# An attention and feed-forward kernel: decay rows in one stacked tile, a K=128 bias matmul for two heads, and a schedule written out as tokens

## The chip, the cores and the metric

The kernel runs on one core of a Trainium2 chip. The metric is the device time of one execution in microseconds (us), lower is better. The span of a profile (first to last instruction) is shorter than the device time of the same run (before: 415.4 against 417.08). In the text, PE is the matmul engine, DVE the vector engine, ACT the scalar engine, POOL the engine that issues the loads of q, k, v and weights, SP the engine that issues most of the other DMAs. The granted clock is the share of its full clock at which PE was allowed to run; "half clock" is a share of 0.5. Warming matmuls are matmuls on constant data that only keep PE busy. A slot is the tile that holds q and k of four heads; `widen` and `narrow` are the two feed-forward layers.

## The reference

Causal attention with a decay bias over 8 batches, 8 heads, 576 positions and 64 dimensions per head, followed by a low-rank mix along the sequence and a feed-forward layer with residual.

```python
scores = (q @ k.T) / sqrt(64)
cum = cumsum(maximum(s, 0), axis=-1)
bias = -(cum[:, :, :, None] - cum[:, :, None, :])
scores = where(causal_mask, -1e9, scores + minimum(bias, 0))
attn = softmax(scores);  x = (attn @ v) with heads side by side     # (8, 576, 512)
h = x.T @ U @ V                                                     # rank 32, along the sequence
u = x + h.T
out = u + maximum(u @ w_ch1, 0) @ w_ch2                             # 512 -> 2048 -> 512
```

## The kernel before

Per head, the scores are matmuls over 68 rows: 64 of q and k and 4 "decay rows" that carry the bias (three bf16 parts of `cum` on k's side against ones, and `-cum` against one). The decay rows of all 64 heads are made by one chain of vector operations at the start. Those of batch 0 are sent to the slots by DMA, those of later batches go through HBM.

```python
# ... s of all 64 heads, one row each: 64 partitions, 144 KB
nc.sync.dma_start(out=s_sb, in_=s.rearrange("b h s -> (b h) s"))
# ... loads of the first q and k are issued on gpsimd
spin(10)                                     # warming matmuls, 512 columns each
nc.vector.tensor_scalar(s_sb, s_sb, 0.0, 1.0 / scale, op0=ALU.max, op1=ALU.mult)
nc.vector.tensor_tensor_scan(cum, s_sb, s_sb, 0.0, op0=ALU.add, op1=ALU.max)
nc.scalar.copy(hi, upper(cum))
nc.vector.tensor_sub(rest, cum, upper(cum))
nc.scalar.mul(rows[:, 3, 0, :], cum, -1.0)
nc.vector.tensor_sub(lo, rest, upper(rest))
nc.vector.tensor_copy(mid, upper(rest))
# ...
for h in range(H):                           # rows of batch 0 into the slots
    send(nc.scalar if h in (1, 3) else nc.sync, h)
```

The rest is generators. Attention of a pair of heads (`scores`, `values`, `mix`) yields at fixed places, and at a given rate a step of feed-forward work is put in there: a quarter of `narrow`'s row block or one of `widen`'s 16 blocks, four 512-column matmuls each. A group of 512 tokens has 32 such steps.

```python
def place(g):                                # q and k of heads 16 and up, four heads at a time
    fetch_rows(g)
    # ... 4 x nc.vector.transpose on (128 x 576), then DMAs to the slot

def attend(n, rate):                         # n: pair of heads
    if n < NP:
        run(scores(n), rate)                 # 4 steps put in
    if n > 2 * PB:
        run(values(n - 1), rate)             # 2 steps
        run(mix(n - 1), rate)                # 1 step: U at once after the values of the same pair
        if hp == 0:
            fill.append(widen(b - 1))

def rest():
    for n in range(2 * PB, NP + 1):
        # ...
        if hp % 2 == 0 and n // 2 + 1 < NP // 2:
            place(n // 2 + 1)                # four transposes in a row on DVE
        attend(n, 1.0)
        if hp == 0:
            fill.append(narrow(b - 1))
```

The opening (batch 0) runs without feed-forward work, with 40 warming matmuls in all; batch 1 runs at rate 0.5 beside the first feed-forward group.

The softmax here doesn't subtract the row's maximum and nothing guards it: scores larger than these inputs give would overflow.

## Time and profile before

| | before |
|---|---|
| device time, median (first three runs) | 416.95 us |
| all runs of it in this study | 413 to 421 us, one at 427 |
| PE busy, of the span | 93% |
| first score matmul | 13.9 us |
| first feed-forward matmul ("first widen") | 44.5 us |
| first score of pair 8 (end of batch 1) | 98.2 us |
| last matmul | 411.4 us |

The page of the profile gives PE's busy tenths in 40 slices of 10.4 us, and the granted clock in tenths.

```profile
PE   7688888899889899999899999999999999999996
...
PEclk9689969999999999999999999999999999999999
```

PE is nearly full from the fifteenth slice (145 us) on. What can be gained lies before that, in idle time and in the slices of low clock. The clock records have two stretches at half: 13.7 to 23.9 and 54.6 to 61.5 us. The records begin only at 6.9 us, and the views count the time before as full; but the first ten warming matmuls start 0.43 us apart and those from 6.86 us on 0.22 us apart, so PE was at half clock until then as well.

The windows view, cut at the three stages (opening, batch 1, rest), has in its columns the length, the busy time of each engine (instructions in brackets), the granted clock, the time of all DMA packets as a share of 16 engines' time (packets overlap, so it can exceed 1) and GB/s.

```profile
core 0: us, PE busy (x) PEld busy (x) DVE busy (x) ACT busy (x) POOL busy (x), PEclk, DMA share, GB/s
0.00:44.51 44.51, 34.16 (x366) 22.04 (x373) 23.63 (x52) 22.79 (x41) 29.94 (x49) 0.88 1.48 160
44.51:98.19 53.68, 47.17 (x422) 27.01 (x429) 28.94 (x59) 24.44 (x49) 28.39 (x44) 0.94 1.25 114
98.19:411.40 313.21, 304.24 (x2548) 170.87 (x2596) 140.73 (x314) 151.94 (x296) 49.64 (x82) 1.00 0.42 74
```

The first stage has 10 us of PE idle, the second 6.5. About 2% of the matmul records are missing in this trace (3335 matmuls against 3396 weight loads), so PE's busy times are a little low, those of the last stage included.

The list of PE's waits (total, how often, longest; us):

```profile
PE pwork L308 <- DVE x_sb L293: 9.2, 8, 1.4
PE pscore L227 <- DMA slot<-hT: 3.5, 1, 3.5
PE pwork L328 <- DVE ux L317: 2.4, 10, 0.7
PE pscore L227 <- ACT pT L241: 2.1, 2, 1.1
```

L308 is the first matmul of the mix, which waits for the division that writes x_sb. Five of its eight waits, 6.1 us, lie in the last stage. The timeline of the opening (start, length, engine, line, what; in square brackets the idle time before and its releaser). From timelines only the lines that matter are shown, here and below:

```profile
0.80 0.59 SPq L444 DMA_DIRECT2D hT<-in_s_dram  x1
3.56 0.45 DVE L474 TENSOR_SCALAR hT<-hT 64x576 f32<-64x576 f32 x1
5.50 0.45 PE L166 MATMUL pwork<-identity,hT 72*128 72x72 bf16 x4
13.93 0.61 PE L227 MATMUL pscore<-slot 68*128 68x128 bf16 x4 [3.50 <-DMA slot<-hT]
```

The first score matmul stands 3.50 us for the rows' DMA, at 13.93.

### The profile page before, as it was taken

How to read it: one execution, taken by the hardware profiler on the slowest of the kernel's cores; microseconds unless marked ns; L12 is line 12 of the kernel's file. 1: busy time of each engine (PE TensorE's matmuls, PEld its weight loads, DVE VectorE, ACT ScalarE, POOL GpSimd, SP SyncE). 2: the span in 40 equal slices, each digit the busy share in tenths (PEclk: the TensorE clock that was granted, in tenths of full speed). 3: DMA queues.
4: the chain of work that ended last, by engine and by line, in shares of the span. 5: the costliest groups of instructions: out<-in, count | busy, mean ns of one | idle time of the engine just before them, and what ended most of it. 6: DMA issues, size and time to landing. Idle time of an engine off the chain costs nothing.

```text
span 415.4 us, 8407 instructions
## 1 busy us (share of the span) xinstructions
PE 385.6 (93%) x3335; PEld 219.9 (53%) x3396; DVE 194.0 (47%) x425; ACT 199.2 (48%) x386; POOL 108.0 (26%) x173
## 2 busy tenths in 40 slices
PE   7688888899889899999899999999999999999996
PEld 3456454555555455555556555565556544444442
DVE  7344355458867557474665843444344401001011
ACT  3373866505762367535663476337743450530610
POOL 8774367347563644053004000000000000000000
PEclk9689969999999999999999999999999999999999
DMA  7999999999986995379119311210001002001002
GB/s 109 189 161 178 195 115 111 74 87 189 233 132 102 180 156 73 71 96 171 28 36 127 100 41 30 69 58 11 2 27 52 25 2 76 28 14 63 25 25 76
DMA packets 76077, 36.75 MB, mean 88 GB/s; under 512 B 61382, under 2 KB 67814, under 8 KB 76038
## 3 DMA queue, kind: packets, MB, share of 16 engines
q0 software_dynamic: 65584, 18.44, 48.9%
q1 hardware_dynamic: 10438, 17.76, 14.2%
q8 instruction: 26, 0.43, 0.4%
q14 instruction: 13, 0.11, 0.1%
q10 hardware_dynamic: 16, 0.02, 0.0%
HBM read 37.51 MB, written 9.95 MB: 114 GB/s over the span
## 4 chain that ended last, share of the span: by engine, by line
PE 66%; DMA 11%; DVE 10%; issue 5%; POOL 4%; ACT 2%; SPq 1%; DVEq 0%; ACTq 0%; POOLq 0%
PE pwork L377 24%; PE pwork L361 23%; PE pscore L227 7%; PE pwork L283 5%; DVE turned L194 4%; DMA qk_sd<-in_k_dram 3%; DMA w_sb<-in_moe_w_ch_dram 2%; DMA slot<-turned 2%; DMA uT<-in_k_dram 2%; PE pwork L308 2%; DVE x_sb L293 2%; PE pwork L388 2%; DVE slot L175 1%; DMA v_slot<-in_v_dram 1%; PE pwork L337 1%
## 5 line engine op out<-in xcount | busy, mean ns | idle before, releaser
L361 PE MATMUL pwork<-uT,w_sb 128*128 128x512 bf16 x548 | 143.0, 382 | 2.0 <-ACT hT L368 0.4
L377 PE MATMUL pwork<-w_sb,hT 128*128 128x512 bf16 x550 | 138.3, 379 | 1.3
L368 ACT ACTIVATE hT<-pwork 128x512 bf16<-128x512 f32 x144 | 88.5, 614 | 83.0 <-PE pwork L361 82.8
L227 PE MATMUL pscore<-slot 68*128 68x128 bf16 (+4 forms) x576 | 70.9, 247 | 7.6 <-DMA slot<-hT 3.5
L241 ACT ACTIVATE pT<-pscore 128x512 bf16<-128x512 f32 x64 | 38.8, 606 | 81.3 <-PE pscore L227 70.7
L361 PEld LDWEIGHTS <-w_sb 128*128 128x128 bf16 x576 | 51.2, 98 | 48.3 <-issue 5.2
L377 PEld LDWEIGHTS <-hT 128*128 128x128 bf16 x576 | 51.2, 97 | 48.1 <-issue 2.1
L227 PEld LDWEIGHTS <-slot 68*128 68x128 bf16 x576 | 43.8, 100 | 38.2 <-issue 5.7
L397 DVE COPY o_sb<-pwork 128x512 f32<-128x512 f32 x36 | 24.8, 688 | 78.7 <-PE pwork L388 78.6
L194 DVE STREAM_TRANSPOSE turned<-qk_sd 128x576 bf16<-128x576 bf16 x48 | 50.3, 1119 | 5.2 <-DMA slot<-turned 2.8
L220 DVE TENSOR_TENSOR pT<-pT,keep 128x512 bf16<-128x512 bf16 (+1 forms) x84 | 27.6, 352 | 46.6 <-ACT pT L241 41.7
L249 ACT ACTIVATE pT<-pscore 128x512 bf16<-128x512 f32 x64 | 39.4, 615 | 13.5 <-PE pscore L227 13.5
L283 PEld LDWEIGHTS <-pT 128*128 128x128 bf16 x960 | 36.8, 98 | 12.7 <-issue 1.1
L253 ACT ACTIVATE pT<-pscore 128x512 bf16<-128x512 f32 x64 | 39.7, 620 | 3.3 <-PE pscore L227 3.3
L131 POOL DMA_DIRECT2D v_slot<-in_v_dram x32 | 28.2, 901 | 45.3 <-PE pwork L283 42.8
L283 PE MATMUL pwork<-v_slot,pT 128*128 128x65 bf16 x960 | 39.3, 194 | 0.7 <-DVE uT L348 0.3
L123 POOL DMA_DIRECT2D qk_sd<-in_q_dram x48 | 27.1, 576 | 47.5 <-DVE turned L194 31.5
L348 DVE CAST uT<-pwork 128x512 bf16<-128x512 f32 x30 | 20.7, 689 | 26.0 <-PE pwork L340 26.0
L293 DVE TENSOR_TENSOR x_sb<-pwork,rec 128x320 bf16<-128x320 f32 x64 | 31.3, 489 | 2.1
L123 POOL DMA_DIRECT2D qk_sd<-in_k_dram x48 | 27.2, 578 | 12.8 <-DMA w_sb<-in_moe_w_ch_dram 7.7
L292 DVE RECIPROCAL rec<-pwork 128x5 f32<-128x5 f32 x64 | 11.8, 185 | 33.9 <-PE pwork L283 33.8
L308 PE MATMUL pwork<-x_sb,U_sb 128*128 128x128 bf16 x160 | 14.4, 220 | 9.2 <-DVE x_sb L293 9.2
(65 smaller groups left out, 216.4 us busy)
## 6 DMA issues: line engine op xcount, KB each, us to landing
out_dram<-o_sb SPq DMA_DIRECT2D x36, 256.0 KB
slot<-turned SPq DMA_DIRECT2D x96, 72.0 KB
w_sb<-in_moe_w_ch_dram POOLq DMA_DIRECT2D x8, 512.0 KB, 13.6
v_slot<-in_v_dram POOLq DMA_DIRECT2D x32, 128.0 KB, 5.8
qk_sd<-in_q_dram POOLq DMA_DIRECT2D x48, 72.0 KB, 3.9
qk_sd<-in_k_dram POOLq DMA_DIRECT2D x48, 72.0 KB, 4.7
uT<-in_q_dram POOLq DMA_DIRECT2D x2, 288.0 KB, 10.4
uT<-in_k_dram POOLq DMA_DIRECT2D x2, 288.0 KB, 11.2
```

The costliest lines, as they stand in the source:

```text
L123: nc.gpsimd.dma_start(out=qk_t[g][ds(32 * a, 32), c, :].rearrange("p (n f) -> p n f", n=6), in_=src[g // 2, 4 * (g % 2) + a].rearrange("(n ...
L131: nc.gpsimd.dma_start(out=vt[:, t, :, 0:D], in_=v[b, :, ds(t * 128, 128), :].rearrange("h p d -> p h d"),)
L194: nc.vector.transpose(turned[:, e, c].rearrange("p (n m t) -> p n t m", n=6, t=3), src[:, c].rearrange("p (n t e d) -> p e n t d", n=6, t= ...
L227: nc.tensor.matmul(dst, lhsT=kT[:, ds(j * 128, 128)], rhs=qT[:, lo:hi], start=start, stop=stop, skip_group_check=not stop,)
L241: nc.scalar.activation(pT[:, hh, 0:512], diag, EXP, scale=scale)
L249: nc.scalar.activation(pT[:, hh, 512:1024], far, EXP, scale=scale)
L253: nc.scalar.activation(pT[:, hh, 1024:1536], mid, EXP, scale=scale)
L283: nc.tensor.matmul(po[:, i, :], lhsT=pT[:, hh, ds(spot(j, i), 128)], rhs=vt[:, j, h, :], start=(j == 0), stop=(j == i), skip_group_check=True,
L293: nc.vector.tensor_tensor(x_sb[:, :, ds(h * D, D)], po[:, :, 0:D], rec.to_broadcast([128, 5, D]), op=ALU.mult,)
L361: nc.tensor.matmul(f1, lhsT=w1_sb[nf // 4][:, kt, ds(nf % 4 * 128, 128)], rhs=uT[:, kt, ds(g * 512, 512)], start=(kt == 0), stop=(kt == 3),)
L368: nc.scalar.activation(hT[:, nf, :], f1, RELU)
L377: nc.tensor.matmul(f2, lhsT=hT[:, nf, ds(i * 128, 128)], rhs=w2_sb[nf // 4][:, nf % 4, :], start=(nf == 0), stop=False, skip_group_check=True,
```

## The change

The intent, as the diff shows it: heads 0 and 1 need not wait for the DMA of their decay rows, because a second matmul over all 128 rows of a stacked tile (4 parts x 32 heads) adds their bias from where the chain leaves it; the chain of heads 32 to 63 is split off and runs later; and the order of everything is written as a list of tokens, so that divisions, mixes and transposes can stand where nothing waits for them. Cut to its core:

```diff
-    TP, TT = 72, 8
+    TP, TT = 96, 6                      # fold of q and k of heads 0 to 15
+    FR = 4 * H
+    def load_decays(i, s_sb):           # 32 heads, four times: 128 partitions, 288 KB
+        nc.sync.dma_start(
+            out=s_sb,
+            in_=bass.AP(s..., i * FR * S, [[0, 4], [S, FR], [1, S]]),
+        )
+    def decays(rows, s_sb, cum):
+        blk = [ds(i * FR, FR) for i in range(4)]
+        # ... the same operations on 128 partitions; part i is written to block i
+    def product(h, dst, j, lo, hi, start, stop):
+        bias = bias_0 if h < 2 else None
+        rows = D if bias else KA
+        nc.tensor.matmul(dst, lhsT=head_of(h)[0:rows, ds(S + j * 128, 128)], ...)
+        if bias:                        # K=128: all parts, this head picked by rhs
+            nc.tensor.matmul(dst, lhsT=bias[0][:, ds(j * 128, 128)],
+                             rhs=bias[1 + h][:, lo:hi], ...)
... (cut)
-        spin(10)                        # 40 warming matmuls in all; 16 after ("p8" twice)
... (cut)
+    SEQ = (
+        "p8 T0 tA0 tV0 T1 tA1 tV1 p8 | Z0 D0 d0 T2 tV2 tV2 E0 f0 m0 D1 d1 T3 tV3 tV3 E1 f1 m1 "
... (cut)
+        "r R3 L0 D8 d8 F r E8 k8 f8 m8 T12 tV12 tV12 D9 d9 F r E9 k9 f9 m9 l4 K4 T13 tV13 "
+        "tA13 F r F r D10 d10 F r E10 k10 f10 m10 T14 tV14 tV14 D11 d11 F r E11 k11 f11 m11 "
... (cut)
+    PAIR = (
+        "D0 d0 U-2 uV-2 X-2 F r E0 k0 f0 G1 m0 F r D1 d1 Y-2 yV-2 F r E1 k1 f1 G1 m1 l0 F r "
+        "A-2 K0 a-2 F r A-1 a-1 F r F r F r "
+    )
```

Tokens: D, E are score matmuls of a head, d, f, m, l its exps; T transposes of a head, tA and tV their copies on ACT or DVE; A values and a their division; U, X, Y parts of a pair's mix and u, y their copies; G one DVE transpose of a later group; F one feed-forward step and r its relu or output copy; L the later decay chain; p warming matmuls. In PAIR the numbers count from the present pair: A-2 and A-1 are the two heads of the pair before, U-2 is the mix of two pairs before. PAIR holds 8 steps F, where the generators took 7 per pair.

## The prediction

> **What bounds it now.** TensorE. The windows view gives it 9.9 of every 10 us busy from 150 us on, at full clock; the last 80 us are feed-forward matmuls alone. It is below that before 150 us: busy 7.5, 6.5, 8.6, 8.6, 8.3 and 7.6 us in the first six tens. PE's list of waits sums to 23 us: 9.2 us of the low-rank mix (L308) on x_sb, 3.5 on the decay rows' DMA, 2.4 on ux, 2.1 on an exp, 1.3 on a slot copy. The granted clock is half in two stretches, about 13.8 to 24.0 and 54.7 to 61.5 us. The Trainium skill, "TensorE: Matmul & The Clock Gate", Part 1, says the clock halves after an idle window of about 3.4 us; the trace agrees: the first stretch begins after 3.5 us of waiting for the rows.
>
> Three stages in the timeline: opening (batch 0) to 44.5, batch 1 with the first feed-forward group 44.5 to 98.2, then 313 us to the last matmul at 411.4.
>
> **What changes.**
> 1. Heads 0 and 1 take the bias from SBUF by a K=128 matmul and wait for no row DMA. It adds 2 x 1600 columns, about 1.4 us of PE at the traced 216 ns per 512 columns. The decay chain (ready at 7.4 us) gains a few small DVE operations. First scores should start near 9.5 instead of 13.9 us.
> 2. But values of head 0 need batch 0's v, whose last load (issued 17.2, 7.1 to landing) is there at 24.3; the load order is kept. They ran at 29.3; now PE, in order, stops there until about 24.5, perhaps with its clock halved again. So about 5 us of gain survive.
> 3. Behind that come about 11 us of PE work, 9.5 of ACT and 12.6 of DVE (0.8 us per head copy, 0.67 per division). I put the first widen at 40 us (37 to 43), against 44.5. Fewer warming matmuls (16, not 40) help.
> 4. Batch 1 with 32 feed-forward steps is about 41 us of PE work (32 x 0.87, plus the rest) and took 53.7. Mixes move behind other matmuls, divisions ahead of copies; I expect 43: 10 us saved, and no half-clock stretch.
> 5. Afterwards U comes two pairs late, so x_sb is ready, and the 1.1 us stream transposes no longer stand before divisions. That removes about 6 us of L308 waits after 98 us. PE work is unchanged.
> 6. A new cost: steady pairs take 8 feed-forward steps, not 7. Counting tokens, the 32 in stock after the sequence are used up in pairs 8 to 11; pair 12 and the first two steps of 13 find none. Pair 12 is then limited by DVE (about 5.8 us against 3.1 of PE). I charge 3 to 5 us, more if the clock halves.
> 7. Later decays: about 5 us of DVE at the end of batch 1, 1 us seen by PE.
>
> **Sum.** 40 + 43 + (313 - 6.5 + 4 + 1) + 4 = 398.5; I say 398 us, 8 in 10 between 390 and 407. Chances: faster 0.93, same 0.05, slower 0.02.
>
> **What would show it.** First score matmul by 10 us; a PE wait of 3 to 6 us for v before 25 us; first widen 37 to 43; batch 1 done at 80 to 86; L308's waits under 2 us; a PE gap of 3 to 5 us around 120 to 130 without feed-forward matmuls; a dense end as before.
>
> **What would make it wrong.** The v wait absent, or costing a long half-clock stretch; rows of heads 2 to 7 landing late; DVE order stalling PE in batch 1; ACT falling behind with 8 steps; the decay chain blocking ACT.

## The result and the profile after

The changed kernel takes 411.88 us (median of 4 runs, 411.83 to 411.92); the kernel before 417.59 (4 runs). The ratio is 0.986, with a 95% interval of 0.983 to 0.989. A ratio here is the mean time of one kernel's fast runs over that of the other's of the same rounds, so it is not quite the ratio of the medians. Repeated, the same kernel gave 412.29. The gain is 1.4%, which by the mark of 2% counts as the same time (the prediction gave that 0.05); 398 us had been predicted.

The page after:

```profile
PE   5999888989999799999999999999999999999996
...
PEclk9858999999999889999999999999999999999999
```

The windows of the three stages after (columns as before):

```profile
0.00:45.74 45.74, 37.63 (x345) 23.14 (x346) 27.02 (x58) 20.72 (x39) 28.64 (x48) 0.81 1.62 165
45.74:94.06 48.32, 42.84 (x413) 25.32 (x412) 27.89 (x62) 24.55 (x49) 23.39 (x38) 1.00 0.90 109
94.06:406.09 312.03, 308.19 (x2602) 174.06 (x2600) 152.64 (x320) 153.88 (x298) 55.34 (x88) 0.99 0.51 77
```

| stage | before | predicted | after |
|---|---|---|---|
| opening, to the first widen | 44.5 | 40 | 45.7 |
| batch 1, to the first score of pair 8 | 53.7 | 43 | 48.3 |
| rest, to the last matmul | 313.2 | 311.5 | 312.0 |

The opening is no shorter. Batch 1 gained half of what was expected. Of its 5.4 us, 0.9 is work that moved: before pair 8 the traces have 128 weight loads of the feed-forward layers in the kernel before and 124 in the changed one, so one step of 32 (0.87 us by the prediction) went from batch 1 to the rest. The rest came out as the sum said, but, as will be seen, by two errors that cancel. The prediction's sum was also a span (40 + 43 + 311.5 + 4 = 398.5) that was given as a device time, which is 1.9 us more.

The opening in the timeline after:

```profile
0.80 0.74 SPq L170 DMA_DIRECT2D hT<-in_s_dram  x1
8.09 0.46 DVE L185 TENSOR_SCALAR hT<-hT 128x576 f32<-128x576 f32 x1 [4.34 <-DMA hT<-in_s_dram]
8.50 1.27 PE L208 MATMUL pwork<-identity,hT 96*128 96x96 bf16 x12 [3.65 <-DMA hT<-in_q_dram]
13.98 0.23 PE L250 MATMUL pscore<-slot 64*128 64x128 bf16 x1 [0.80 <-DVE slot L220]
```

s is used at 8.09 instead of 3.56 us and the first transposes run at 8.50 instead of 5.50. The 4.4 us that the bias matmul was to save were lost before it: the first score comes at 13.98, as before. The stretch at half clock runs from 17.2 to 34.2 us, 17 us instead of 10. Here the clock records begin at 13.8 us, and all 16 warming matmuls before it start 0.43 us apart: of its first 34 us the changed kernel had 3.4 at full clock, where the kernel before had 6.8 of its first 24.

PE's waits after:

```profile
PE pwork L359 <- DVE x_sb L345: 5.6, 5, 2.5
PE pwork L208 <- DMA hT<-in_q_dram: 3.6, 1, 3.6
PE pscore L250 <- ACT pT L315: 1.9, 2, 1.2
PE pwork L414 <- DVE uT L404: 1.3, 5, 0.5
...
PE pwork L329 <- ACT slot L220: 1.2, 1, 1.2
```

The mix (L359 now) no longer waits in steady pairs, and the wait for the rows' DMA is gone. New are the wait of 3.6 us for the first q, one of 2.5 us (the longest of L359's), and waits on an exp and on a slot copy in batch 1. The long wait of L359 is the place that the prediction called dry, here in the timeline of PE:

```profile
137.42 0.42 PE L250 MATMUL pscore<-slot 68*128 68x128 bf16 x5
140.30 0.69 PE L359 MATMUL pwork<-x_sb,U_sb 128*128 128x128 bf16 x5 [2.46 <-DVE x_sb L345]
...
143.10 1.89 PE L414 MATMUL pwork<-uT,w_sb 128*128 128x512 bf16 x4
```

Between 134.8 and 143.1 us there is no feed-forward matmul; the prediction had put the gap at 120 to 130. Four matmuls of 512 columns take 1.89 us at 143.10 against 1.03 elsewhere: the clock was at half from 140.1 to 146.9 us.

### The profile page after: what moved, and what is told of

Read it like the earlier page. It is cut to its first block, busy times and chain, and to the rows that moved or that the text cites. A ratio compares the mean times of both kernels' runs of the same rounds, so it can differ in the third digit from the quotient of the medians.

```text
span 410.0 us, 8377 instructions
## 1 busy us (share of the span) xinstructions
PE 388.7 (95%) x3358; PEld 222.5 (54%) x3358; DVE 208.2 (51%) x439; ACT 199.1 (49%) x386; POOL 107.4 (26%) x173
## 4 chain that ended last, share of the span: by engine, by line
PE 85%; DVE 8%; DMA 3%; ACT 2%; POOL 1%; issue 1%; DVEq 0%
PE pwork L414 29%; PE pwork L431 28%; PE pscore L250 11%; PE pwork L329 6%; PE pwork L359 2%; PE pwork L443 2%; DMA hT<-in_s_dram 2%; PE pwork L377 2%; DVE turned L234 2%; PE pwork L397 1%; DVE o_sb L454 1%; DVE uT L404 1%; DVE x_sb L345 1%; PE pscore L259 1%; PE pwork L208 1%; DMA v_slot<-in_v_dram 1%
## 5 line engine op out<-in xcount | busy, mean ns | idle before, releaser
L315 ACT ACTIVATE pT<-pscore 128x512 bf16<-128x512 f32 (+1 forms) x224 | 112.4, 558 | 85.9 <-PE pscore L250 74.2
L414 PE MATMUL pwork<-uT,w_sb 128*128 128x512 bf16 x576 | 140.8, 382 | 1.3 <-DVE uT L404 1.3
L431 PE MATMUL pwork<-w_sb,hT 128*128 128x512 bf16 x576 | 140.4, 379 | 0.0
L421 ACT ACTIVATE hT<-pwork 128x512 bf16<-128x512 f32 x144 | 86.4, 602 | 74.8 <-PE pwork L414 74.0
L250 PE MATMUL pscore<-slot 68*128 68x128 bf16 (+5 forms) x576 | 72.6, 250 | 2.8 <-ACT pT L315 1.9
L250 PEld LDWEIGHTS <-slot 68*128 68x128 bf16 (+1 forms) x576 | 45.2, 101 | 37.6 <-issue 8.5
L234 DVE STREAM_TRANSPOSE turned<-qk_sd 128x576 bf16<-128x576 bf16 x48 | 54.5, 1138 | 0.7
L318 DVE TENSOR_TENSOR pT<-pT,keep 128x512 bf16<-128x512 bf16 (+1 forms) x84 | 29.8, 355 | 28.2 <-ACT pT L315 27.3
L370 DVE CAST ux<-pwork 128x128 bf16<-128x128 f32 x30 | 8.7, 290 | 48.1 <-PE pwork L359 48.1
L404 DVE CAST uT<-pwork 128x512 bf16<-128x512 f32 x30 | 20.5, 684 | 14.2 <-PE pwork L397 14.2
L220 DVE COPY slot<-pwork 64x576 bf16<-64x576 bf16 x25 | 19.8, 797 | 9.3 <-PE pwork L208 9.0
L359 PE MATMUL pwork<-x_sb,U_sb 128*128 128x128 bf16 x160 | 14.5, 222 | 5.6 <-DVE x_sb L345 5.6
```

The lines of the kernel that those rows point to most:

```text
L234: nc.vector.transpose(turned[:, e, c].rearrange("p (n m t) -> p n t m", n=6, t=3), src[:, c].rearrange("p (n t e d) -> p e n t d", n=6, t= ...
L250: nc.tensor.matmul(dst, lhsT=head_of(h)[0:rows, ds(S + j * 128, 128)], rhs=head_of(h)[0:rows, lo:hi], start=start, stop=stop and not bias, ...
L315: nc.scalar.activation(dst, src, EXP, scale=scale)
L318: nc.vector.tensor_tensor(p, p, m, op=ALU.min)
L414: nc.tensor.matmul(f1, lhsT=w1_sb[nf // 4][:, kt, ds(nf % 4 * 128, 128)], rhs=uT[:, kt, ds(g * 512, 512)], start=(kt == 0), stop=(kt == 3),)
L421: pending.append(lambda nf=nf, f1=f1: nc.scalar.activation(hT[:, nf, :], f1, RELU))
```

## The experiments

All variants start from the changed kernel unless said otherwise, and all gave correct results. Times are medians of four runs (six for the last). The stages below are from one profiled execution each and are cut as above. Runs whose opening was not touched (the changed kernel twice, the stock and the copies) had openings of 45.7, 46.8, 47.0 and 47.4 us, so openings are good to 1.7 us only, and that of the changed kernel's first profile is the shortest of the four; batch 1 and the rest repeat to 0.3 us unless a half-clock stretch falls into them.

| run | what | opening | batch 1 | rest | time |
|---|---|---|---|---|---|
| before | | 44.5 | 53.7 | 313.2 | 417.6 |
| after | | 45.7 | 48.3 | 312.0 | 411.9 |
| after_again | unedited | 46.8 | 49.4 | 311.6 | 412.3 |
| one_copy | s loaded once | 41.2 | 48.3 | 311.8 | 407.3 |
| fold72 | fold of 72 x 8 | 47.6 | 48.4 | 312.0 | 413.5 |
| s_four | s in four DMAs | 44.8 | 48.4 | 310.5 | 410.6 |
| rows_dma | no K=128 bias | 45.5 | 48.4 | 311.6 | 411.9 |
| warm_early | 12 more warming matmuls at the start | 47.4 | 48.4 | 311.7 | 412.4 |
| warm22_again | 22 warming matmuls in batch 0 | 49.9 | 49.5 | 311.7 | 416.2 |
| stock | 6 steps in pairs 8 to 12 | 47.0 | 48.3 | 304.9 | 406.3 |
| copies_dve | three copies on DVE | 47.4 | 45.3 | 311.9 | 409.4 |
| combo | one_copy + stock + copies_dve | 41.3 | 45.3 | 304.7 | 397.0 |
| combo_rows | combo, no K=128 bias | 40.1 | 45.3 | 304.7 | 396.1 |
| combo_mix | combo, later mixes in batch 1 | 41.3 | 42.2 | 304.3 | 394.3 |
| best | combo_mix, no K=128 bias, one division earlier | 38.5 | 42.4 | 305.0 | 391.6 |

**The control.** The changed kernel once more, unedited.

> The changed kernel itself once more, unedited, on the chip of this call: a control, since its times come from another call than those of its variants. If variants may be compared across calls to 1 us: 411 to 413, first widen 45 to 48 us depending on where the half-clock stretch starts. If its time moves by more than 2 us, the verdicts on 2 us differences (the copies) fall.

412.29 us (411.79 to 413.6). Its batch 1 is 1 us longer; a half-clock stretch fell on 45.8 to 49.2 us. Variants may be compared across calls to about 1 us.

### The opening

**one_copy: load s once.** The four blocks of the stacked tile can be written from the same 32 partitions, so the fourfold load is not needed.

```diff
-                [[0, 4], [S, FR], [1, S]],
+                [[S, FR], [1, S]],
...
+        s_sb, cum = s_sb[:FR], cum[:FR]
-        nc.scalar.mul(rows[blk[3], 0, :], cum[blk[3]], -1.0)
+        nc.scalar.mul(rows[blk[3], 0, :], cum, -1.0)
... (the other three writes alike)
```

> Edit: s is loaded once (32 rows, 72 KB) instead of four times (288 KB); the same vector operations write the four blocks of rows from the 32 partitions. Correct result. Theory A (the fourfold load of s is what ate the opening's gain: it shares the DMA engines with the first q and k, so s lands at 8.1 us and the first q at 8.5): s lands by 4 us, the first transposes run by 6 us, the first score matmul by 10.5 us instead of 14.0, and the half-clock stretch begins later or is shorter; first widen at 40 to 43 us instead of 45.8; time 406 to 409. Rival B (the 96-row fold of q and k makes their loads slow): first transposes stay after 7.5 us, first score after 12 us, time within 1 us of 411.9. Rival C (the opening is bound by its half clock, whatever starts it): first score early, but first widen still after 45 us, time 410.5 to 412.5.

407.26 us. Its timeline:

```profile
3.68 0.54 DVE L186 TENSOR_SCALAR hT<-hT 32x576 f32<-32x576 f32 x1
4.92 0.42 PE L209 MATMUL pwork<-identity,hT 96*128 96x96 bf16 x3
9.52 0.23 PE L251 MATMUL pscore<-slot 64*128 64x128 bf16 x1 [1.43 <-DVE slot L221]
```

s is used at 3.68, the transposes run at 4.92, and the first score comes at 9.52, which is the 9.5 us of the prediction. The first widen follows at 41.2 (predicted 40). Theory A holds but for the clock: the half-clock stretch begins earlier and is as long as in the changed kernel (12.0 to 29.1). Theory C does not hold: the whole opening moved forward by 4.5 us.

**fold72: put the fold of q and k back.**

```diff
-    TP, TT = 96, 6
+    TP, TT = 72, 8
```

> Edit: the fold of q and k for heads 0 to 15 is put back from 96 rows of 6 to 72 rows of 8, all else as after. Theory A (the load of s): nothing much moves; s still lands near 8 us, first transposes after 7.5 us, first score near 14, time within 1.5 us of 411.9. Rival B (the fold): first transposes by 6 us, s by 5, first score by 11 us, time 406 to 410.

413.5 us; s is used at 8.31 and the first transposes run at 8.83 us. The fold has no part in it: rival B falls. The time lies 0.1 us over the range given for theory A, with a half-clock stretch of 27 us in the profiled run (8.8 to 36.1).

**s_four: the same 288 KB in four DMAs.** In the view of DMA queues, the share of 16 engines' time that the packets of SP's queue (q1) took, first of the kernel before between 2 and 3 us, then of the changed kernel between 3 and 4 us:

```profile
q1 hardware_dynamic: 80, 0.15, 52.3%
```

```profile
q1 hardware_dynamic: 42, 0.10, 26.3%
```

The columns are packets, MB and share. The stacked load keeps 26% of 16 engines busy, about 4 engines; between 4 and 7 us it is 24%. The Trainium skill, "DMA: Bandwidth & Descriptors", section "Why a DMA increments its semaphore by 16 and not by 1", under "How many engines (k)", says that a DMA is spread over the largest k up to 16 that divides the slowest dimension of both its patterns. The source pattern here begins with a repeat of 4, so k would be 4, which fits the 26%. The packets fit it too: in the first 9 us the queue has 80 before, 64 of 2304 bytes and 16 of 4, and 132 in the changed kernel, 128 and only 4 of 4 bytes, with four in flight for 3.7 of their 4.5 us. So the load was split into four plain ones of the same bytes:

```diff
-        nc.sync.dma_start(out=s_sb, in_=bass.AP(..., [[0, 4], [S, FR], [1, S]]))
+        for a in range(4):
+            nc.sync.dma_start(out=s_sb[ds(a * FR, FR)],
+                              in_=s.rearrange("b h s -> (b h) s")[ds(i * FR, FR)])
```

> Edit: the same 288 KB of s, loaded as four DMAs of 32 rows instead of one DMA whose source pattern begins with a repeat of 4; all else as the changed kernel. Theory P (the single stacked DMA runs on only 4 of the 16 DMA engines: its packets take 24 to 26% of 16 engines' time between 3 and 7 us, the kernel before's took 52% for under 1.5 us): s lands by 4.5 to 5.5 us (the fourth issue ends near 3), first q by 6.5, first score 10 to 11.5 us, time 407 to 409.5, nearly all of the single load's gain. Rival Q (it is the 288 KB that cost, sharing the engines with q and k): s still lands after 7 us, first score after 13 us, time 410.5 to 413.

```profile
5.30 0.42 PE L205 MATMUL pwork<-identity,hT 96*128 96x96 bf16 x3 [0.44 <-DMA hT<-in_q_dram]
5.54 0.68 DVE L182 TENSOR_SCALAR hT<-hT 128x576 f32<-128x576 f32 x1 [1.79 <-DMA hT<-in_s_dram]
```

The first q is there at 5.30, as fast as before the change, and s is used at 5.54 instead of 8.09 us, though the bytes are the same. The queue took 49% of the engines' time between 2 and 3 us. So of the 4.4 us by which s came later than in one_copy (8.09 against 3.68), 2.55 go to the pattern and 1.86 to the bytes and the three more issues (at least: in one_copy DVE came to s at 3.68 without waiting for it). The time, 410.63, does not decide: it lies in the range of rival Q, the first score (11.8) lies between the two, and the gain of about 1.3 us is near the scatter. In the profiled run (409.53) the opening is 0.9 us shorter, with 20.5 us at half clock, and the rest 1.5, where the half clock of the dry pair lasted 3.4 us instead of 6.8. So the pattern is shown as the larger part of the delay of s, not of the 4.6 us that one_copy gained.

**rows_dma: undo the K=128 bias.**

```diff
-        bias = bias_0 if h < 2 else None
+        bias = None
-        for h in range(2, H):
+        for h in range(H):              # all rows of batch 0 by DMA
```

> Edit: the K=128 bias matmul for heads 0 and 1 is undone: all eight heads of batch 0 get their rows by DMA from the stacked tile, all else (fourfold load of s, schedule) as after. If the K=128 matmul is worth what I predicted (it removes the wait for the row DMA, about 4 us of first score), the first score comes at 15.5 to 18.5 us instead of 14.0, and the opening gets longer by 1 to 4 us less the 1.4 us (2.8 at half clock) of bias matmuls: first widen at 45 to 48, time 411 to 415. If it is worth nothing because PE is at half clock and the bias matmuls are paid double, first widen 43.5 to 45.5, time 409.5 to 411.

411.92 us: no difference. The time lies in the range that was given for a matmul that pays (411 to 415), but so does that of the changed kernel, and the first score (19.2) comes later than either case had it. What decides is when the values start. First the changed kernel: scores (L250) and bias matmuls (L259) of head 0 at full clock and of head 1 at half clock, the first scores of head 2, the first values matmul. Then the first scores, those of head 2 and the first values of this run:

```profile
14.14 0.23 PE L259 MATMUL pscore<-hT 128*128 128x128 bf16 x1
14.30 0.23 PE L250 MATMUL pscore<-slot 64*128 64x128 bf16 x1
17.99 0.29 PE L250 MATMUL pscore<-slot 64*128 64x128 bf16 x1
18.21 0.29 PE L259 MATMUL pscore<-hT 128*128 128x128 bf16 x1
24.06 0.63 PE L250 MATMUL pscore<-slot 68*128 68x128 bf16 x4
29.56 1.01 PE L329 MATMUL pwork<-v_slot,pT 128*128 128x65 bf16 x15
```

```profile
19.19 0.59 PE L250 MATMUL pscore<-slot 68*128 68x128 bf16 x4 [6.01 <-DMA slot<-hT]
24.22 0.63 PE L250 MATMUL pscore<-slot 68*128 68x128 bf16 x4
29.72 1.01 PE L329 MATMUL pwork<-v_slot,pT 128*128 128x65 bf16 x15
```

The scores start 5.2 us later, and the values of head 0 still start at the same time. From the first score to the first of head 2 the two heads take 10.1 us in the changed kernel and 5.0 here: the bias matmuls cost 5 us of PE, not "about 1.4". Alternating with scores, with weights loaded for each, matmuls of 128 columns start 0.16 us apart at full clock and 0.22 at half. Without the alternation they start 0.06 apart at full clock (four in 0.23 us at 35.7) and 0.11 at half (four in 0.42 at 24.06). The prediction's figure is the 0.06, so the half clock is the smaller part of the miss. Why the alternation is so slow no run tests. The two heads paid in PE time what they saved in waiting.

**warm22 and warm_early: warming matmuls.** Two theories of the half clock. In the first, 22 warming matmuls go back among the scores and values of batch 0 (the edit also moves the warming matmuls to another PSUM tile):

```diff
-        "... D0 d0 T2 tV2 tV2 E0 f0 m0 D1 d1 ..."
+        "... D0 d0 p1 T2 tV2 tV2 E0 f0 m0 p1 D1 d1 p1 ..."   # and so on to m7
```

> Edit: 22 warming matmuls (512 columns each, into a spare PSUM tile) put back between the scores and values of batch 0, where the kernel before had them. Theory D (their removal lengthened the half-clock stretch from 10.2 to 17.1 us and so cost the opening time): the stretch shrinks to about 10 us, first widen at 43 to 45 us instead of 45.8, time 409 to 411. Rival E (the stretch has another cause, or PE's rate does not bound the opening): the stretch stays 17 us, the 22 matmuls cost 4.7 to 9.4 us of PE, first widen at 47 to 54 us, time 413 to 419.

Its fast runs took 414.2 to 419.8 us, the profiled run 510.7 us at a clock of 0.749.

> The kernel with 22 warming matmuls once more, because its profile fell in the slow state. If the matmuls do shorten the half-clock stretch in the fast state, it is 10 us or less and first widen comes by 45 us, which would overturn the verdict from its times; if they do not, the stretch is 13 us or more, first widen at 47 to 54 us, time 413 to 419 as before.

416.23 us. The stretches at half clock are 8.2 to 11.6, 15.0 to 32.1 and 49.1 to 52.5 us; the middle one is 17 us, as without the matmuls, and the first widen comes at 49.9. Theory D falls: their removal is not what made the stretch longer, and leaving them out is a gain of about 4 us.

In the second, PE is kept busy while it waits for the first q:

```diff
-        "p8 T0 tA0 tV0 T1 tA1 tV1 p8 | ..."
+        "p20 T0 tA0 tV0 T1 tA1 tV1 p8 | ..."
```

> Edit: 20 warming matmuls instead of 8 ahead of the first transposes, so that PE is kept busy while it waits for the first q (4.9 to 8.5 us). Theory H (that idle stretch starts the half clock, and the half clock bounds the opening): the half-clock stretch of 17 us is gone or under 7 us, first widen at 40 to 43 us instead of 45.8, time 407 to 410. Rival I (the clock goes to half later anyway because the scores of batch 0 keep PE too lightly busy, or ACT and DVE bind at full clock): a stretch of 10 us or more is still there before 36 us, or first widen stays at 45 to 46.5; time 411 to 413.

412.42 us; the stretch begins earlier than without (14.8) and lasts to 35.3. Rival I holds as to the result. What ends the stretch stays open. The Trainium skill, "TensorE: Matmul & The Clock Gate", Part 1, says that about 3.4 us of sustained activity release the clock; in this run and in the changed kernel PE was busy 10.00 of 10 us from 24 to 34 us, by the windows view, and the clock stayed at half.

### Batch 1

In the timeline of DVE, ACT and PE of the changed kernel, L220 is the copy of transposes to the slot:

```profile
56.39 0.79 DVE L220 COPY slot<-pwork 64x576 bf16<-64x576 bf16 x1
57.21 0.80 ACT L220 COPY slot<-pwork 64x576 bf16<-64x576 bf16 x1 [1.11 <-DVE slot L220]
59.66 0.41 PE L250 MATMUL pscore<-slot 68*128 68x128 bf16 x5 [1.18 <-ACT pT L315]
```

The token pair tV13 tA13 sends the two copies of a head to DVE and ACT. The ACT copy starts only when the DVE copy ends (its releaser in the brackets), and ACT, in order, stands 1.11 us idle with exps behind it; PE then waits 1.18 us for an exp. Heads 11 and 15 do the same.

```diff
-    T11 tV11 tA11 ... T13 tV13 tA13 ... T15 tV15 tA15
+    T11 tV11 tV11 ... T13 tV13 tV13 ... T15 tV15 tV15
```

> Edit: the second copies of heads 11, 13 and 15 go to DVE instead of ACT. Theory J (each such copy on ACT waits about 1 us for the DVE copy of the same head, because both write the same stretch of the slot, and holds up the exps behind it; PE then waits 0.67, 1.18 and 1.22 us): these three PE waits fall under 0.3 us each, batch 1 (first widen to first score of pair 8) takes 45 to 46.5 us instead of 48.5, time 409 to 410.5. Rival K (DVE is the scarcer engine there): the waits move to x_sb, batch 1 stays over 47.5, time 411 to 413.

409.43 us, batch 1 45.3 us instead of 48.3. PE's waits in batch 1 are then these:

```profile
PE pwork L359 <- DVE x_sb L345: 2.2, 2, 1.7
PE pwork L377 <- DVE x_sb L345: 0.6, 1, 0.6
PE pwork L377 <- DVE uT L404: 0.6, 1, 0.6
```

The waits on exps and on the ACT copy are gone; the one on x_sb grew from 1.1 to 2.2 us. Theory J holds, with a little of rival K. What is left are U and X standing too close behind the division of the same pair. That was tried later, on the combination.

### The rest

**stock: fewer steps in pairs 8 to 12.**

```diff
+    FEW = PAIR.replace("F r F r F r ", "F r ")        # 6 steps F instead of 8
-            play(PAIR, n)
+            play(PAIR if n > 12 else FEW, n)
```

> Edit: pairs 8 to 12 take 6 feed-forward steps each instead of 8, so that the stock lasts until the next group is queued; from pair 13 on 8 as before. Theory F (the dry pair 12 costs its DVE-bound wait and a half-clock stretch of 6.8 us, 3.4 us of PE, together about 5.7 us): no gap near 138 us, no half clock after 50 us, time 405.5 to 407.5. Rival G (the dry pair's work had to be done anyway and ACT or DVE now bind in pairs 8 to 12): the gap is spread over these pairs, time 409 to 412.

406.29 us. The gap is gone, no half clock falls after 50 us, and the rest takes 304.9 us:

```profile
95.32:400.19 304.87, 304.15 (x2602) 172.17 (x2600) 151.91 (x320) 153.85 (x298) 55.32 (x88) 1.00 0.52 79
```

PE is busy 304.15 of 304.87 us. Theory F holds, its estimate included (5.6 us by the times). By the stage, the dry pair cost 312.0 - 304.9 = 7.1 us; the profiled stock run had an opening 1.2 us longer than the changed kernel's, which is in its time. The later decay chain cost nothing that PE shows: between 90 and 100 us of the changed kernel, where DVE ran it, PE was busy 9.99 of 10.

### Together

**combo:** the edits of one_copy, stock and copies_dve.

> Edit: s loaded once, 6 steps in pairs 8 to 12, and the three copies on DVE, together; correct result. If the three costs are independent, 411.9 - 4.6 (measured for the single load) - 5.6 (measured for the stock) - 2 (expected for the copies) = 399.7: 398.5 to 402. If the copies give nothing: 401 to 402.5. If the gains overlap: over 403.

396.99 us (396.87 to 397.26), ratio 0.954 against the kernel before. By the stages the three costs add up (the sum of the times, 399.2, is 2.2 us higher, with openings of stock and copies_dve that happened to be longer), and without them the kernel lands within 1 us of the 398 predicted (in part by chance, since the terms that were off in the other direction, such as the gain in the rest, are still in it).

**combo_rows:** the combination with the K=128 bias undone, edit as in rows_dma.

> Edit: the combination with the K=128 bias undone (all rows of batch 0 by DMA). Theory L (at half clock the bias matmuls cost 2.4 us per head, as the trace of the changed kernel shows, about what the row DMA's wait costs): first score at 13 to 16 us instead of 9.5, yet values of head 0 within 1 us of 25.5 and first widen within 1 us of 41.3; time 396 to 398. Rival M (with s early, the K=128 matmul pays as I predicted): values of head 0 after 27.5, first widen after 43 us, time 399 to 402.

396.09 us. First score at 13.4 instead of 9.5 us, values of head 0 at 24.0 instead of 25.5, first widen at 40.1 instead of 41.3. The time fits theory L; the values and the first widen come 1.5 and 1.2 us earlier, a little outside its range and away from rival M: with s early too, the K=128 matmul costs about 1 us (the scatter between calls is as large).

**combo_mix:** the mixes of batch 1 behind one more step.

```diff
-    D12 d12 U4 uV4 X4 F r E12 k12 f12 m12 D13 d13 Y4 yV4 F r E13
+    D12 d12 F r E12 k12 f12 m12 U4 uV4 X4 D13 d13 F r Y4 yV4 E13
... (pairs 5, 6 and 7 alike; two steps F taken from the end of SEQ)
```

> Edit: the combination with the mixes of batch 1 one feed-forward step later, same number of steps. Theory N (what is left of PE's waits in batch 1, 1.65 + 0.56 + 0.60 + 0.57 us, is U and X standing right behind the division they need): these waits fall under 0.3 us each, batch 1 is 2.5 to 3.4 us shorter, time 393.5 to 395. Rival O (the waits come back at another matmul, because a held PSUM tile or DVE binds): time 395.5 to 397.5.

394.29 us; batch 1 takes 42.2 us. In PE's list of waits for batch 1 one line is left:

```profile
PE pwork L415 <- DVE slot L221: 0.4, 1, 0.4
```

Theory N holds.

**best:** combo_mix without the K=128 bias, and with the division of head 7 ahead of the copies of head 8.

```diff
-    Y2 yA2 T8 tV8 tV8 A7 a7 T9 tV9 tV9 Z1 U3
+    Y2 yA2 T8 A7 a7 tV8 tV8 T9 tV9 tV9 Z1 U3
```

> Edit: the combination with later mixes, plus the K=128 bias undone, plus the division of head 7 ahead of the copies of head 8 in the opening (PE waited 1.38 us there for x_sb). If these are independent: 394.3 - 0.9 (measured for the undone bias on the combination) - 1.2 = 392.2, 391.5 to 393.5, faster than both kernels. If the division gives nothing, because the copies then come late for batch 1: 393 to 394.

391.55 us (390.22 to 391.88), as expected for independent gains; ratio 0.940 (0.934 to 0.945) against the kernel before: faster than both kernels, by 25 and 20 us of the medians.

```profile
0.00:38.47 38.47, 29.68 (x328) 20.64 (x328) 23.88 (x51) 20.50 (x39) 27.55 (x46) 0.82 1.47 164
38.47:80.89 42.42, 41.75 (x414) 25.05 (x413) 31.71 (x67) 22.67 (x46) 23.00 (x39) 1.00 1.19 141
80.89:385.89 305.00, 304.07 (x2602) 172.24 (x2600) 151.79 (x320) 153.87 (x298) 57.18 (x89) 1.00 0.54 79
```

In the last two stages PE is busy for all but 1.6 us. (The cut at 38.47 is the first weight load; its matmul starts at 38.93.)

## Why the prediction was wrong

The direction was right and the size was not: 411.9 us against 398, outside the range of 390 to 407. Between the sum of 398.5 and the result lie 5.7 us in the opening, 5.3 in batch 1, 0.5 in the rest and 1.9 for the span given as a time.

1. **Step 1, "First scores should start near 9.5 instead of 13.9 us": failed.** The step took the chain's start from the kernel before (s ready at 3.6 us) and costed only the added vector operations. The term left out was the load itself: the stacked tile is filled by a DMA of twice the bytes, whose pattern begins with 4 and which ran on about 4 of 16 DMA engines. s came 4.5 us late and the first q 3 us. With s loaded once, the first score came at 9.52 us and the opening took 41.2 (shown by one_copy; that the pattern has the larger part of the delay of s is shown by the arrival times in s_four). That 41.2 is so near the 40 of the prediction is in part luck, by points 2 and 3.
2. **The K=128 bias, "about 1.4 us of PE": mis-sized.** It took 5 us (rows_dma), because matmuls that alternate with the scores start 0.16 us apart at full clock and 0.22 at half, where 0.06 had been booked for 128 columns, and undoing it changed nothing in the changed kernel (411.9 both) and gained 0.9 us in the combination.
3. **Step 2, a stop for v of batch 0: did not show.** PE's list has no wait for v in any opening. In one_copy the values of head 0 started at 25.4 us, near the 24.5 of the prediction, but because PE took that long over the scores. In combo_rows they started at 24.0, without a wait for v.
4. **Step 4, "I expect 43: 10 us saved": failed in size.** It gained 5.4 us, 0.9 of it by one step less. "Divisions ahead of copies, mixes behind other matmuls" was read from the tokens without asking of each how far ahead it stood. Copies split between DVE and ACT hold up ACT (3.0 us, shown by copies_dve), and mixes stand too close behind their divisions (3.2 us more, shown by combo_mix). With both put right, batch 1 takes 42.2 us. The forecast that no half-clock stretch would fall here held in most runs; in after_again one did.
5. **Steps 5 and 6, the rest: right by cancellation.** The mechanism of both was right. The late U removed the 6.1 us of waits and the stage gained 313.2 - 304.9 = 8.3 us once the dry pair was filled, where 5.5 had been booked; some 1.7 us of it (2.6 with the step that moved here) were not traced to listed waits. The dry pair cost 7.1 us instead of 3 to 5: the half clock that the text had named as "more if" did come, for 6.8 us.
6. **Step 7, the later chain:** 1 us was charged, none was seen.
7. **The clock.** Keeping the half clock away was not achieved by any run, and what ends the stretch in the opening, of 13.7 us in best to 27.3 in fold72 and stock, is open. Neither warming matmuls in between nor keeping PE busy ahead of it shortened it. The prediction put the start of a stretch down to an idle gap of about 3.4 us. That fits the first one of the kernel before (3.5 us), but in the changed kernel the clock fell at 17.2 us with no gap of PE above 0.8 us since 8.5, and in the kernel before at 54.6 with none above 1.3 us in the 14 us ahead of it. What starts a stretch is open too.

## What to carry to other kernels

When a tile is laid out anew so that an on-chip step becomes cheaper, cost the load that fills it as well: its bytes, the number of engines it spreads over, and what it delays in the same queue time. A schedule written by hand has to be counted to the end (here 33 steps are in stock at pair 8, 8 are taken per pair, and the next are queued only after the second step of pair 13); here the gap cost its own wait of 2.5 us and then 6.8 us at half clock. And a matmul added to hide a wait should be costed at the pace at which it runs in its place: here it ran at 0.16 to 0.22 us instead of 0.06, and cost all that it saved.

## What the Trainium skill lacked or had wrong

- "TensorE: Matmul & The Clock Gate", Part 1, gives about 3.4 us of sustained activity as what releases the clock. In the opening of the changed kernel PE was 100% busy by the profile from 20 to 34 us and stayed at half clock for 17.1 us; in other runs the stretch was 13.7 to 27.3 us. The matmuls themselves ran slowly in it (512 columns took 0.63 us at 32.95 and 0.38 at 35.94), so this is no error of the clock records.
- No page gives what it costs to alternate matmuls over 64 and over 128 rows: of 128 columns they start 0.16 us apart at full clock, 0.22 at half, against 0.06 and 0.11 for scores alone.
- Not lacking: "DMA: Bandwidth & Descriptors" has the rule on the number of engines of a DMA, and the runs agree (24 to 28% of 16 engines for a pattern that begins with 4, 49 to 52% for the plain loads). Its section "Rules for kernel authors" also warns of a leading broadcast of c copies, which confines a DMA to at most c engines; here such a load of 288 KB took 7.3 us from issue to use.
